# x of pair 0 through SyncE's queue as float32, first weights behind pair 0's C, GpSimd's other loads spread out

## The chip, the cores and the metric

The kernel runs on one core of one Trainium2 chip. The time is device microseconds of one execution. The core has five engines that run side by side: TensorE (PE in the profile, its weight loads PEld), VectorE (DVE), ScalarE (ACT), GpSimd (POOL) and SyncE (SP). SyncE, ScalarE and GpSimd issue DMAs; each has a queue of its own, and all queues run on the same 16 DMA engines. Of the three, only GpSimd's DMAs change the type of the data on the way.

## The reference

Two parts follow each other. The first is a chunked state-space recurrence (Mamba2) over x, a, B and C with 4 batches, 8 heads, 768 tokens, head width 32 and state width 16. The second is a bilinear feed-forward layer on its result, with 3,072 tokens, 256 model columns and 1,536 hidden columns.

```python
for c in range(S // chunk):
    cum = np.cumsum(la, axis=-1)                       # la: log of a in this chunk
    L = np.exp(cum[:, :, :, None] - cum[:, :, None, :]) * causal
    y_intra = ((Cc @ Bc^T) * L) @ xc
    y_inter = (Cc @ state) * np.exp(cum)[..., None]
    y[:, :, sl] = y_intra + y_inter
    state = np.exp(la.sum(-1)) * state + sum_j decay_j * outer(Bc_j, xc_j)
...
x2 = y.transpose(0, 2, 1, 3).reshape(B * S, H * D)
out = ((x2 @ w_a) * (x2 @ w_b)) @ w_out
```

## The kernel before, in words

The kernel takes chunks of 128 tokens: six blocks, and in each block two pairs of batches, so that pair p is block p // 2 and batches 2 (p % 2) and the one after it. Pairs 0 and 1 (block 0) start the work and have a path of their own; pairs 2 and 3 (block 1) and the later ones follow with other layouts.

For a pair of block 0 the work is this. `load1` brings B, C or x of one batch (64 partitions of two tokens each). `scan` on VectorE makes the running products of a; `factors_mm` and a reciprocal turn them into factors per token. `scale_bc` multiplies B or C with its factor into float16 (tiles bm and cm). `transposes` turns bm and cm on TensorE, VectorE and ScalarE copy the result to bt and ct. `scores` forms B times C in four banks (SC), `mask` multiplies them with the causal table: three quarters on VectorE, one by a ScalarE copy to tmp and a GpSimd product. `pv_u` multiplies the masked scores with x (tile X16, called xn in the profile), and `evac0` or `pv1` copies the result to X2T. Then the feed-forward part begins on TensorE: `unit_mm` multiplies X2T with a slice of Wa or Wb, `evac_a` copies the first product, `times` multiplies the two, `out_mm` multiplies with Wo. Warm-up products of constants fill TensorE's early gaps.

The order of instructions on each engine is written out by hand; no scheduler moves them. An engine runs its list in order and waits where an instruction's inputs are not there. The loads at the start are spread over the queues as follows:

- SyncE: a, then of pair 0 half of B and a quarter of C, then of pair 1 half of C and half of B. Later `load_q(1)`, C and B of block 1 in eight DMAs (tiles cq and bq), which wait until the first Wa has landed; then x of pairs 2 and 3 as float32 (`load_x32`, cast by ScalarE at L723), B of pairs 2 and 3, and block 2.
- ScalarE: the other half of B, half of C and a quarter of C of pair 0 (L198, rows 32 to 63 of batch 0), and the other halves of C and B of pair 1.
- GpSimd, after it has built the identity and the causal table: x of pair 0 in two DMAs, cast to float16 on the way, the first half of Wa (`w0`) and of Wb, x of pair 1 in two DMAs, the second half of Wa. It then computes `mid_rows(0, 1)` (tile Ps, used from the first `turned_rows` on) and its share of pair 0's mask, clears two tiles and issues the second half of Wb.

The weights are float32 in memory and are cast to float16 by GpSimd's queue. The columns of a half that a unit uses: units 0 to 2 of each pair use the first half of Wa and Wb, units 3 to 5 the second.

The DMAs of SyncE and ScalarE share eight completion semaphores in turn, so an issue waits until the DMA eight places before it, in the order of the program, has landed.

Of the kernel before, what the change touches and what calls it, by code (L numbers as in the profile page):

```python
# [10 lines left out]
f32 = mybir.dt.float32  # L11
# [5 lines left out]
AFTER = mybir.DependencyInfo(mybir.DependencyClass.Sync, mybir.DependencyReason.DATA)  # L17
# [11 lines left out]
def kernel(  # L29
# [13 lines left out]
    nc = tc.nc  # L43

    nb, H, S, D = x.shape
# [32 lines left out]
    Wa = [big.tile([128, 2, KC], f16, name=f"Wa{t}") for t in range(2)]  # L78
    Wb = [big.tile([128, 2, KC], f16, name=f"Wb{t}") for t in range(2)]
# [27 lines left out]
    in32 = ctx.enter_context(tc.tile_pool(name="in32", bufs=2))  # L107
# [16 lines left out]
    st = {}  # L124
# [4 lines left out]
    def bank(name):  # L129
        return psf.tile([128, 512], f32, name=name, tag=f"ff{next(banks)}")  # L130
# [9 lines left out]
    def by_token(t_):  # L140
        return t_.rearrange("p h r n -> p (h r n)").rearrange("p (t h n) -> p t h n", t=2, h=H)

    def load1(eng, p, which, bt, i0=0, n=64, to=None):
        blk, bp = divmod(p, NBP)
        if p >= P2:
            return eng.dma_start(
                by_token(pair_in[p][which])[:, bt],
                (B, C, x)[which][2 * bp + bt, :, blk * Q : (blk + 1) * Q, :].rearrange("h q n -> q h n"),
            )
        src = (B, C, x)[which][2 * bp + bt, :, blk * Q + 2 * i0 : blk * Q + 2 * i0 + 2 * n, :]  # L150
        if to is None:
            to = pair_in[p][which]
        return eng.dma_start(  # L153
            to[64 * bt + i0 : 64 * bt + i0 + n].rearrange("i h r n -> i h (r n)"),
            src.rearrange("h (i r) n -> i h (r n)", r=2),
        )
# [23 lines left out]
    def load_w(half, W):  # L180
        src = moe_w_a if W is Wa else moe_w_b
        c = slice(half * KC, (half + 1) * KC)
        return nc.gpsimd.dma_start(W[half], src.rearrange("(f p) e -> p f e", p=128)[:, :, c])

    def load_wo(half):
# [2 lines left out]
            moe_w_out.rearrange("(g p kk) e -> p g (kk e)", p=128, kk=3)[:, 2 * half : 2 * half + 2],  # L188
        )

    nc.sync.dma_start(a_sb, a.rearrange("b h (k q) -> (b h) k q", q=Q))
    for p_ in range(2):
        tiles(p_)
# [1 line left out]
    load1(nc.sync, 0, 0, 0)  # L195
    load1(nc.scalar, 0, 1, 1)
    load1(nc.sync, 0, 1, 0, 0, 32)
    load1(nc.scalar, 0, 1, 0, 32, 32)  # L198
    for w in (1, 0):
        load1(nc.sync, 1, w, 0)  # L200
        load1(nc.scalar, 1, w, 1)
# [19 lines left out]
    for bt in range(2):  # L221
# [1 line left out]
        nc.gpsimd.affine_select(  # L223
            out=v, in_=v, compare_op=ALU.is_ge, fill=0.0, base=0, pattern=[[-1, 2], [1, Q]], channel_multiplier=-2
        )
    for p in range(2):
        for bt in range(2):
            load1(nc.gpsimd, p, 2, bt)
        if p == 0:
            w0 = load_w(0, Wa)  # L230
            load_w(0, Wb)
    load_w(1, Wa)

    def warmup(bank, *widths):
        for cols in widths:
            nc.tensor.matmul(
                bank[:, 0:cols],
                nc.const_aps.tensor(1.0, [128, 128], mybir.dt.bfloat16),
                nc.const_aps.tensor(1.0, [128, cols], mybir.dt.bfloat16),
                start=True,  # L240
                stop=True,
                skip_group_check=True,
            )


    def scan(lo, hi):
        for k in range(lo, hi):
            nc.vector.tensor_tensor_scan(Pr[:, k], a_sb[:, k], zero, 1.0, ALU.mult, ALU.add)
# [4 lines left out]
    def sel_over_mid(lo, hi, eng):  # L253
        eng.tensor_tensor(
            out=selr[:, lo:hi].rearrange("p k t c -> p k (t c)"),
            in0=sel.rearrange("p t b h -> p (t b h)").unsqueeze(1).broadcast_to((BH, hi - lo, 2 * NBP * H)),
            in1=rmid[:, lo:hi].unsqueeze(2).broadcast_to((BH, hi - lo, 2 * NBP * H)),
            op=ALU.mult,
        )
# [24 lines left out]
    def mid_rows(lo, hi, eng):  # L284
        k = slice(lo + NBLK - NT, hi + NBLK - NT)
        eng.tensor_tensor(
            out=Ps[:, lo:hi], in0=Pr[:, k], in1=rmid[:, k].unsqueeze(2).broadcast_to((BH, hi - lo, Q)), op=ALU.mult
        )

    def clear(t_, eng):  # L290
        words = t_.rearrange("p c s -> p (c s)").bitcast(u32).rearrange("p (g w) -> p g w", g=3)
        eng.memset(words[:, 0:2, 32:96], 0)
# [23 lines left out]
    def flat(f, lo, hi):  # L316
        return f[:, lo:hi].rearrange("p k r b h -> p (k r b h)")
# [47 lines left out]
    def transposes(p, ps=None, between=None, apart=False):  # L365
        s = st[p]
        if ps is None and apart:
            ps = [SC[0], SC[1]]
        TB, TC = (TT[:, 0:256], TT[:, 256:512]) if ps is None else [t_.bitcast(f16)[:, 0:256] for t_ in ps]
        for T_, src in ((TB, s["bm"]), (TC, s["cm"])):  # L370
            for r in range(2):
                nc.tensor.transpose(
                    T_[:, r * 128 : (r + 1) * 128], src[:, r].rearrange("p h n -> p (h n)"), ident
                )
            if between:
                between()
                between = None
        BT = mid.tile([128, 2, 2, Q], f16, name="bt", tag="bt")
        CT = mid.tile([128, 2, Q], f16, name="ct", tag="ct")
        co, ci = CT.rearrange("p t q -> p (t q)"), TC  # L380
        if p < P2:
            co, ci = CT.rearrange("p t (i r) -> p r (t i)", r=2), TC.rearrange("p (r c) -> p r c", r=2)
        b_ = nc.vector.tensor_tensor(
            out=BT.rearrange("p e r k -> p e (r k)"),
            in0=TB.unsqueeze(1).broadcast_to((128, 2, 256)),
            in1=par.unsqueeze(2).broadcast_to((128, 2, 256)),
            op=ALU.mult,
        )
        c_ = nc.scalar.copy(co, ci)
        if apart:  # L390
            tc.declare_no_dep(c_.ins, b_.ins.name, reason="reads of two banks")
        if p < P2:
            BT = BT.rearrange("p e r (t i) -> p e r t i", t=2)
        s["BT"], s["CT"] = BT, CT
# [37 lines left out]
    def product0(m2, e):  # L432

        return (
            st[0]["T1"][:, 2 * m2 : 2 * m2 + 2].rearrange("p m (e r) q -> p e m (r q)", e=2)[:, e],
            (SC0, SC1)[m2][:, :, e * 256 : e * 256 + 256],
            causal.rearrange("p r q -> p (r q)").unsqueeze(1).broadcast_to((128, 2, 2 * Q)),
        )

    def mask(out_in, by_pool=False):  # L440
        o_, i_, c_ = out_in
        if by_pool:
            tmp = mid.tile([128, *c_.shape[1:]], f32, name="tmp", tag="tmp")
            nc.scalar.copy(tmp, i_)  # L444
            nc.gpsimd.tensor_tensor(out=o_, in0=tmp, in1=c_, op=ALU.mult)  # L445
        else:
            nc.vector.tensor_tensor(out=o_, in0=i_, in1=c_, op=ALU.mult)  # L447
# [176 lines left out]
    def unit(p, k2, between=None, by_pool=False):  # L624
        a_ps = unit_mm(p, k2, Wa)
        if between:
            between()
        b_ps = unit_mm(p, k2, Wb)
        asb = evac_a(a_ps)
        return lambda: times(p, k2, b_ps, asb, by_pool)  # L630
# [85 lines left out]
        if blk < NBLK:  # L716
            load_q(nc.sync, blk)

    def load_x32(p):
        x32 = in32.tile([128, H, 2, D], f32, name="x32", tag="x32")  # L720
        for bt in range(2):
            load1(nc.sync, p, 2, bt, to=x32)
        return lambda: nc.scalar.copy(  # L723
            st[p]["X16"].rearrange("p h r d -> p (h r d)"), x32.rearrange("p h r d -> p (h r d)")
        )

    def loads_x(p):
        if p < NP:
            load2(nc.gpsimd, p, 2)
# [52 lines left out]
    scale_bc(0, 1, nc.vector, v.rearrange("p (r b h) -> p r b h", r=2, b=NBP)[:, :, 0])  # L782
    over_mid(1, 2)
    sel_over_mid(1, 2, nc.vector)
    mid_rows(0, 1, nc.gpsimd)
    tb, tcp = bank("tb"), bank("tc")
    transposes(0, [tb, tcp], lambda: warmup(SC[3], 256))
    nc.scalar.copy(flat(fC, 0, 1), v)
    scan(3, 4)
    warmup(SC[3], 512, 512)  # L790
    scores(0)
# [1 line left out]
    mask(product0(0, 1))  # L793
    mask(product0(1, 1), by_pool=True)
    mask(product0(1, 0))
    clear(planes[0], nc.gpsimd)
    warmup(tcp, 512)
    factors_mm(1, 2, fps, 1)
# [16 lines left out]
    for p in (2, 3):  # L815
        tiles(p)
    x_in = [load_x32(p) for p in (2, 3)]
    for p in (2, 3):
        load2(nc.sync, p, 0)
# [72 lines left out]
    h = unit(1, 4, lambda: scores(2))  # L892
# [32 lines left out]
    for c in range(3):  # L925
        p, bt = divmod(c, NBP)
# [135 lines left out]
```

## Time and profile before

| what | value |
|---|---|
| time, median of 3 runs | 123.13 us (122.97 to 123.83) |
| the profiled execution | 123.47 us, of which the span of the instructions is 121.8 us |
| granted TensorE clock | 1.00 |
| TensorE busy | 116.0 us, 95% of the span |
| VectorE, ScalarE, GpSimd busy | 90.3, 66.7, 58.6 us |
| chain that ended last | PE 68%, DMA 15%, SPq 10%, POOL 3% |
| GpSimd's queue (q0) | 20,256 packets, 3.67 MB |
| SyncE's queue (q1) | 36,976 packets, 7.87 MB |
| ScalarE's queue (q10) | 2,528 packets, 0.36 MB |

How to read the profile: the page cuts the span into 40 equal slices of 3.05 us and gives each engine's busy share of a slice in tenths. The chain of work that ended last is followed back from the last instruction, at each step to what released it. The timeline lists instructions in order of time, alike ones merged, each with its start, its duration, its engine ("SPq", "ACTq" are issues by a queue's engine, not work), its line and its tiles, and in brackets the idle time of the engine before it and what ended that. Line numbers are those of the kernel before; the times are from the start of the span. The DMA view of a stretch of time gives for each queue the packets that started in it, their bytes in MB and the time that they took as a share of 16 engines.

### The profile page before, as it was taken

Reading aid. Unit: us, or ns where it says so; the run is one execution under the profiler, and the core shown is the slowest. Engines: PE = TensorE matmul, PEld = TensorE weight load, DVE = VectorE, ACT = ScalarE, POOL = GpSimd, SP = SyncE. Lnnn points to the kernel's source line nnn. Section 1 sums busy time; section 2 is a strip of 40 time slices with the busy share of each in tenths; the row PEclk is TensorE's granted clock in tenths of the full one; section 3 lists DMA queues with packets and bytes.
Section 4 is the critical chain, followed back from the end, with each engine's and each line's share of the span. In section 5 each row is a group of like instructions: output and inputs, shape, how many; then the busy total and the mean of one; then the engine's idle time right before and its main releaser. Section 6 shows DMA issues by size and latency. Waiting matters only on the chain.

```text
span 121.8 us, 3551 instructions
## 1 busy us (share of the span) xinstructions
PE 116.0 (95%) x1385; PEld 73.6 (60%) x1386; DVE 90.3 (74%) x167; ACT 66.7 (55%) x131; POOL 58.6 (48%) x94
## 2 busy tenths in 40 slices
PE   7889899999999999999999999999999999999990
PEld 2336689888734468644476464766464684655880
DVE  5998986999888995599966989686799345748000
ACT  0446746668567654567656637545645537565220
POOL 7994876987769999395901995200000000000000
DMA  3999999993488999999992909212001012010122
GB/s 65 131 172 193 205 200 181 172 201 73 102 85 98 168 104 107 123 78 114 197 309 95 95 0 122 12 46 86 5 0 43 12 51 74 0 43 0 43 97 81
DMA packets 59777, 12.13 MB, mean 100 GB/s; under 512 B 54992, under 2 KB 59728, under 8 KB 59760
## 3 DMA queue, kind: packets, MB, share of 16 engines
q0 software_dynamic: 20256, 3.67, 42.8%
q1 hardware_dynamic: 36976, 7.87, 35.8%
q10 hardware_dynamic: 2528, 0.36, 1.8%
q8 instruction: 11, 0.18, 0.7%
q14 instruction: 6, 0.05, 0.2%
HBM read 12.42 MB, written 3.15 MB: 128 GB/s over the span
## 4 chain that ended last, share of the span: by engine, by line
PE 68%; DMA 15%; SPq 10%; POOL 3%; issue 1%; DVE 0%; ACT 0%; POOLq 0%
PE ops L691 22%; PE aps L665 20%; PE bps L665 20%; DMA cq<-in_C_dram 7%; SPq L161 5%; DMA Wa<-in_moe_w_a_dram 5%; SPq L153 4%; DMA bq<-in_B_dram 3%; PE SC L402 2%; PE SC L471 2%; POOL xn L153 1%; PE SC L534 1%; POOL causal L223 1%; POOL planes L344 1%; DVE turned L357 0%
## 5 line engine op out<-in xcount | busy, mean ns | idle before, releaser
L610 ACT COPY asb<-aps 128x512 f32<-128x512 f32 x72 | 41.9, 587 | 18.3 <-PE aps L665 13.9
L677 DVE TENSOR_TENSOR hkb<-bps,asb 128x512 f16<-128x512 f32 x60 | 40.1, 685 | 12.4 <-ACT asb L610 11.3
L665 PE MATMUL bps<-XB,Wb 128*128 128x512 f16 x120 | 35.7, 379 | 0.2 <-ACT asb L610 0.2
L665 PE MATMUL aps<-XB,Wa 128*128 128x512 f16 x120 | 35.7, 379 | 0.0
L691 PE MATMUL ops<-Wo,hkb 128*128 128x256 f16 (+1 forms) x252 | 28.1, 268 | 0.0
L691 PEld LDWEIGHTS <-hkb 128*128 128x128 f16 x252 | 23.0, 98 | 3.8
L665 PEld LDWEIGHTS <-Wb 128*128 128x128 f16 x120 | 12.4, 103 | 13.9 <-issue 0.5
L665 PEld LDWEIGHTS <-Wa 128*128 128x128 f16 x120 | 12.1, 103 | 11.7 <-issue 0.5
L447 DVE TENSOR_TENSOR t<-SC,causal_q 128x512 f16<-128x512 f32 x27 | 17.3, 681 | 2.4 <-PE SC L402 2.4
L703 ACT ACTIVATE osb<-ops 128x256 f32<-128x256 f32 (+1 forms) x20 | 7.6, 380 | 18.4 <-PE ops L691 18.4
L445 POOL TENSOR_TENSOR t<-tmp,causal_q 128x512 f16<-128x512 f32 x5 | 5.8, 1160 | 8.8 <-ACT tmp L444 8.8
L175 POOL DMA_DIRECT2D xn<-in_x_dram x8 | 9.5, 1193 | 0.0
L344 POOL TENSOR_TENSOR planes<-bq,FB 128x256 f16<-128x256 f32 x10 | 7.7, 774 | 1.6 <-DMA bq<-in_B_dram 1.5
L620 DVE TENSOR_TENSOR hk<-bps,asb 128x512 f16<-128x512 f32 x11 | 7.3, 677 | 1.6 <-ACT asb L610 0.9
L344 POOL TENSOR_TENSOR planes<-cq,FC 128x256 f16<-128x256 f32 x10 | 7.6, 775 | 1.3 <-DMA cq<-in_C_dram 1.1
L447 DVE TENSOR_TENSOR t<-SC,causal 128x512 f16<-128x512 f32 x11 | 7.0, 676 | 0.4 <-PE SC L402 0.3
L596 PE MATMUL aps<-X2T,Wa 128*128 128x256 f16 x48 | 6.8, 274 | 0.3 <-ACT G L858 0.3
L444 ACT COPY tmp<-SC 128x512 f32<-128x512 f32 x10 | 5.9, 589 | 1.8 <-PE SC L402 1.4
L556 ACT ACTIVATE XB<-SC 128x512 f16<-128x512 f32 (+1 forms) x9 | 4.6, 548 | 4.1 <-PE SC L499 2.4
L596 PE MATMUL bps<-X2T,Wb 128*128 128x256 f16 x48 | 6.6, 273 | 0.0
L445 POOL TENSOR_TENSOR t<-tmp,causal 128x512 f16<-128x512 f32 x5 | 5.7, 1157 | 0.6 <-ACT tmp L444 0.5
L357 DVE STREAM_TRANSPOSE turned<-planes 128x384 f32<-128x384 f32 x10 | 5.5, 564 | 0.5 <-POOL planes L344 0.5
(100 smaller groups left out, 107.3 us busy)
## 6 DMA issues: line engine op xcount, KB each, us to landing
out_dram<-osb SPq DMA_DIRECT2D x23, 128.0 KB, 2.0
cq<-in_C_dram SPq DMA_DIRECT2D x20, 64.0 KB, 4.1
bq<-in_B_dram SPq DMA_DIRECT2D x20, 64.0 KB, 4.0
bn<-in_B_dram SPq DMA_DIRECT2D x8, 128.0 KB, 4.8
xn<-in_x_dram POOLq DMA_DIRECT2D x8, 128.0 KB, 5.7
Wa<-in_moe_w_a_dram POOLq DMA_DIRECT2D x2, 384.0 KB, 7.9
Wb<-in_moe_w_b_dram POOLq DMA_DIRECT2D x2, 384.0 KB, 8.5
Wo<-in_moe_w_out_dram POOLq DMA_DIRECT2D x2, 384.0 KB, 5.8
```

What stands on the lines that cost most here:

```text
L153: return eng.dma_start(to[64 * bt + i0 : 64 * bt + i0 + n].rearrange("i h r n -> i h (r n)"), src.rearrange("h (i r) n -> i h (r n)", r=2),)
L175: eng.dma_start(by_token(pair_in[p][which]).rearrange("p t h n -> p (t h) n"), src.rearrange("t h q n -> q (t h) n"))
L344: eng.tensor_tensor(out=plane[:, c0 : c0 + 4 * step].rearrange("p (j c) s -> p j s c", c=step)[:, :, :, 0:N], in0=by_batch[blk][which][:, ...
L445: nc.gpsimd.tensor_tensor(out=o_, in0=tmp, in1=c_, op=ALU.mult)
L447: nc.vector.tensor_tensor(out=o_, in0=i_, in1=c_, op=ALU.mult)
L596: nc.tensor.matmul(ps[:, kk * 2 * Q : (kk + 1) * 2 * Q], W[k // 6][:, f, k % 6 // 3 * 384 : (k % 6 // 3 + 1) * 384].rearrange("p (c kk) -> ...
L610: (nc.vector.tensor_copy if on_dve else nc.scalar.copy)(asb, a_ps)
L620: eng.tensor_tensor(out=s["hk"][:, 2 * k2 : 2 * k2 + 2, :].rearrange("p k q -> p (k q)"), in0=b_ps, in1=asb, op=ALU.mult)
L665: nc.tensor.matmul(t_, W[k // 6][:, f, k % 6 // 3 * 384 : (k % 6 // 3 + 1) * 384].rearrange("p (c kk) -> p kk c", kk=3)[:, k % 3], XB[:, b ...
L677: return lambda: nc.vector.tensor_tensor(out=s["hk"][:, k], in0=ps[1], in1=asb, op=ALU.mult)
L691: nc.tensor.matmul(o_ps[:, 0:w], hk[:, k, c * Q : (c + 1) * Q], Wo[:, k, cs], start=(k == 0), stop=(k == NK - 1), skip_group_check=True,)
L703: nc.scalar.activation(out=o_sb[:, 0:w], in_=o_ps[:, 0:w], func=AF.Copy, scale=1.0 / (YS * YS))
```

## The change

`load_x32` is moved up, and x of pair 0 goes through it: two DMAs of SyncE's queue into a float32 tile, right behind SyncE's quarter of C of pair 0 and ahead of its halves of C and B of pair 1. The cast to float16 (`x0()`) becomes a ScalarE copy between the copy to fC and the copy to tmp of pair 0's mask. On GpSimd, the first half of Wa waits until ScalarE's quarter of C of pair 0 (`c0`) has landed; behind it come the first half of Wb and the first x DMA of pair 1. The second x DMA of pair 1, the second half of Wa and `mid_rows(0, 1)` stand behind GpSimd's mask of pair 0. The work on VectorE and TensorE keeps its order.

```diff
+    def load_x32(p):
+        x32 = in32.tile([128, H, 2, D], f32, name="x32", tag="x32")
+        for bt in range(2):
+            load1(nc.sync, p, 2, bt, to=x32)
+        return lambda: nc.scalar.copy(
+            st[p]["X16"].rearrange("p h r d -> p (h r d)"), x32.rearrange("p h r d -> p (h r d)")
+        )
...
     load1(nc.sync, 0, 1, 0, 0, 32)
-    load1(nc.scalar, 0, 1, 0, 32, 32)
+    c0 = load1(nc.scalar, 0, 1, 0, 32, 32)
+    x0 = load_x32(0)
     for w in (1, 0):
         load1(nc.sync, 1, w, 0)
         load1(nc.scalar, 1, w, 1)
...
-    for p in range(2):
-        for bt in range(2):
-            load1(nc.gpsimd, p, 2, bt)
-        if p == 0:
-            w0 = load_w(0, Wa)
-            load_w(0, Wb)
-    load_w(1, Wa)
+    w0 = load_w(0, Wa)
+    tc.add_manual_dep(w0.ins, c0.ins.name, AFTER, reason="first weights behind pair 0")
+    load_w(0, Wb)
+    load1(nc.gpsimd, 1, 2, 0)
...
-    mid_rows(0, 1, nc.gpsimd)
     tb, tcp = bank("tb"), bank("tc")
     transposes(0, [tb, tcp], lambda: warmup(SC[3], 256))
     nc.scalar.copy(flat(fC, 0, 1), v)
+    x0()
     scan(3, 4)
...
     mask(product0(1, 0))
+    load1(nc.gpsimd, 1, 2, 1)
+    load_w(1, Wa)
+    mid_rows(0, 1, nc.gpsimd)
     clear(planes[0], nc.gpsimd)
```

More of the change, by code (lines that the diff above doesn't have):

```diff
@@ L717, in loads_q @@
             load_q(nc.sync, blk)
[L719 to L725, printed above, removed]
     def loads_x(p):
```

## The prediction

> **What bounds the kernel now.** I read the page's slices of the span first, then the chain of waits, then the timeline up to 38 us, then the DMA queues by windows.
>
> The slices show two stages. The DMA engines are full from about 3 to 28 us; TensorE is busy to the end.
>
> ```profile
> PE   7889899999999999999999999999999999999990
> DMA  3999999993488999999992909212001012010122
> ```
>
> The chain that ended last runs through the DMA queues before it is TensorE alone:
>
> ```profile
> 2.56 1.49 POOL xn L153 x2
> 4.06 6.40 DMA Wa<-in_moe_w_a_dram
> 10.46 0.02 issue
> 10.47 0.32 SPq L161
> 10.79 0.04 issue
> 10.84 8.20 DMA cq<-in_C_dram
> ...
> 30.96 3.40 DMA bq<-in_B_dram
> ```
>
> From 35.92 us on its pieces are matmuls back to back, so a change in the first 10 us reaches the end only through what TensorE loses or regains before that. The timeline shows the point where three things arrive together (columns: start, duration, engine, line, operation, tiles, idle time before with its releaser):
>
> ```profile
> 3.32 0.64 SPq L153 DMA_DIRECT2D bn<-in_B_dram  x1
> 3.60 0.65 ACTq L153 DMA_DIRECT2D bn<-in_B_dram  x1
> 7.17 0.59 ACT L444 COPY tmp<-SC 128x512 f32<-128x512 f32 x1 [0.62 <-PE SC L402]
> 9.89 0.43 DVE L331 TENSOR_TENSOR bm<-bn,fB 128x256 f16<-128x256 f32 x1
> 10.24 0.28 DVE L563 TENSOR_SCALAR X2T<-py 128x128 f16<-128x128 f32 x1
> 10.37 0.11 PEld L372 LDWEIGHTS <-bm 128*128 128x128 f16 x2 [0.66 <-DVE bm L331]
> 10.56 0.81 PEld L596 LDWEIGHTS <-Wa 128*128 128x128 f16 x8
> 22.53 0.48 PEld L402 LDWEIGHTS <-turned 32*64 32x64 f16 x32 [0.38 <-DVE turned L357]
> ```
>
> B of pair 1 is scaled at 9.89: ScalarE's half of it, issued at 3.60, took 6.3 us and landed at 9.87; SyncE's half, issued at 3.32, took 4.4 us. Pair 1's transposes wait for it at 10.37. Wa (4.06 + 6.4 = 10.46) arrives when X2T is ready (10.52). So **pair 1's B and the first weights are due at the same moment, with 0.1 us to spare**.
>
> Last, how queues share the engines. In 24 to 26 us GpSimd's queue carried the second half of Wo and SyncE's carried B:
>
> ```profile
> q0 software_dynamic: 213, 0.33, 96.2%
> q1 hardware_dynamic: 203, 0.03, 16.5%
> ```
>
> One for one, though a weight packet (1,536 B, 134 ns in the trace's packet records) lasts ten times a 128 B one (13 ns). SyncE's queue gets 102 packets a us there; from 14.0 to 15.5 us it is 135 against 178, 90 a us. Alone, from 26.4 to 27.4, it moved 1,521 in one us. **Rows of B behind weights move some fifteen times slower than rows without them.**
>
> **The change, part by part.**
>
> *x of pair 0.* Removed from GpSimd's queue: two issues (0.87 and 0.69 us) and 1,024 packets that last 31 ns each with the cast; added to SyncE's: two issues of 0.64 us (what x of pair 2 takes, at L153) and 1,024 packets of 256 B at 20 to 22 ns (805 passed between 22 and 23 us). That is 1,024 x 10 ns / 16 engines = 0.64 us less DMA work. The issues stand at 2.67 and 3.35, where C and B of pair 1 stood; the packets follow C's at 4.4. Beside ScalarE's queue (1,024 packets of B and C at 13 ns) they need (1,024 x 20 + 1,024 x 13) ns / 16 = 2.1 us, so x lands about 6.5 to 7.0.
>
> The cast on ScalarE is one copy of 128x512 to float16, 0.62 us (the two at L723 lasted 614 and 621 ns). It stands ahead of the copy to tmp at 7.17, behind which idle time of 0.62 us shows: it fits if x lands by 6.55; a landing at 7.0 holds tmp, and with it GpSimd's mask, back by 0.45 us. That mask ran 8.01 to 9.16, since mid_rows (7.65, 0.39 us) stood before it; mid_rows now comes after, worth 0.25. Together 0 to +0.2 us on the second half of pair 0, covered by the later wait below; without that cover it would cost up to 0.2.
>
> *Pair 1 behind x.* An issue on SyncE or ScalarE waits for the landing of the DMA eight before it (the waits of SyncE's queue show it: x of pairs 2 and 3 at L153 waits for cq, 2.6 us in all). SyncE's C of pair 1 thus waits for ScalarE's C of pair 0 (1.54 + 3.1 = 4.63) and goes out at 4.65 instead of 2.67; B goes out at 5.33 instead of 3.32, **2.0 us later**.
>
> *First weights behind C of pair 0.* That half C is issued at 2.23 and takes 2.7: it lands at 4.98. Wa goes out at 5.05 instead of 4.06. GpSimd has nothing queued behind this wait that is due before the mask near 8. A weight DMA's first packet comes 1.5 us after its issue (Wo: 16.89 to 18.36, 21.68 to 23.21), so at 6.55. Before it was 6.6, since Wa queued behind x. So weights start when they did; with x gone from their queue they fill it sooner, Wa landing about 9.8 and Wb 11.9 instead of 12.48.
>
> *Where they meet.* B's rows from SyncE cannot start before 5.33 + 1.5 = 6.8 (1.5 is 0.81 to 2.30, first packet of ScalarE's B). Weights are then on the engines, 512 packets of Wa and Wb without a break. I let 100 of B's 512 packets slip through while the weights come up; 412 at 102 a us take 4.0 us; 0.5 more to land (last packet 9.39, landing 9.87, for ScalarE's half) makes 11.3, and up to 0.6 for the tail of C ahead of it: **11.6 us against 9.87, +1.75**. Bounds: weights half a us slower to come up, and B lands near 9.4, at no cost; half of C's 512 rows also caught, and it is 13.0 (+3.1; behind Wb come x's 128 B packets, which let the rest through). I take 11.6, as the 203 and 135 packets are of just this meeting.
>
> *What stands behind it.* On VectorE the scaling at 9.89 is followed by X2T (10.24) and bt (10.81); on TensorE the transposes are followed by pair 0's first products. All slip by 1.75: bt, scores(1), three masks, pv1, X2T, the products of pair 1 at 15.08. TensorE has no long wait from there to 22.15. At 22.53 it waits 0.38 us for turned, which hangs on cq and on GpSimd (idle 1.14 us before 19.89), not on pair 1: that 0.38 is given back. Near 35.9 I count 0.1 more, as bq's landing at 34.36 does not move with pair 1. GpSimd's other issues (x of pair 1's second half at 9.2, Wa's second half at 9.9 instead of 6.83, Wb's at 11.6 instead of 9.40) cost nothing: their queue has Wa, Wb and x ahead until about 12.5, and the products that need them begin at 18.33 and 19.64, against landings of 16.3 and 18.8 before.
>
> **Sum:** 1.75 - 0.38 - 0.1 = +1.25 us. The profiled execution took 123.47 us (span 121.8 and 1.7 around it); it would take 124.7. The median of the three runs is 0.34 lower, 123.13, so I forecast **124.4 us**.
>
> One page speaks to the meeting. The Trainium skill, "DMA: Bandwidth & Descriptors", section "Queues, rings and completion order", says that an engine goes round its queues a packet at a time, a packet being typically some 9 to 17 descriptors. If B's small rows went in such groups, B's 32 rows per engine would pass in two to four turns and be on time (the first rival below). The 213 against 203 records of 24 to 26 us say one row a turn.
>
> **Rivals.**
>
> *Pair 1 in time, a small gain.* For it: weights come up slowly where small packets are still about (87 records of their queue from 7 to 8 us, against 286 in the two us after 8.5), and ScalarE's halves of C and B no longer meet x's cast packets. It decides if B lands by 9.9. Then what is left is 0.64 us of DMA work, of which TensorE can take back the 0.38 before scores(2): 123.13 - 0.4 = 122.7. Against it: 1,521 rows a us fell to 102 in the one meeting of B with weights, and SyncE's B took 5.7 to 6.4 us there; from 5.33 that is 11.0 to 11.7.
>
> *C and B both caught.* C's rows from SyncE (4.65 + 1.5 = 6.15) stand behind x's until about 6.3. If x ends 0.4 later, half of C goes at the slow rate too, and B lands at 13.0: +3.1 - 0.5 = +2.6, 125.7 us. It decides once C lands after 8.98, when VectorE scales it. For it: cq, issued into weights at 10.47, had its first packet only at 14.07. Against it: the C halves of pair 1 took 3.9 us before, and 4.65 + 3.9 = 8.55.
>
> *x too late for its users.* If x landed after 8.0, pair 0's products at 8.17 would wait. Until 11.6 that is hidden behind B's wait, so it changes no number unless the first rival holds, where it costs up to 0.5: 123.2.
>
> **How the numbers follow.** Forecast 0.55, the first rival 0.30 (with the late x in it), the second 0.15. A measurement of this kernel tells about 1% (1.2 us) from no change. The forecast's +1.25 lies on that edge: of its 0.55, 0.36 is slower by over 1% (B at 11.6 or later, or less given back), 0.19 within. The first rival is within 1% for 0.25; 0.05 is left for faster, since the gain would have to exceed all DMA work saved. The second is slower. That gives 0.05, 0.44, 0.51. The range runs from 122.7, the first rival, to 125.8, just over the second.
>
> **What would show it.** Right: SyncE's C and B of pair 1 issued near 4.65 and 5.33; Wa near 5.05; B's issue to landing 5.7 us or more; the scaling of B at L337 near 11.6 and the transposes behind it, with TensorE idle over 1 us there; the wait of 0.38 at scores(2) gone; x's cast near 6.6 to 7.2. Wrong: B landed before 9.9, or a wait after 12 us that grew (for Wb, cq or turned), or a gap of TensorE after 22 us that took the delay up.

## The result and the profile after

The changed kernel takes 124.84 us (median of 11 runs, 123.72 to 125.21) against 123.37 us of the kernel before on the same chip (11 runs): a ratio of 1.0096, 95% interval 1.0072 to 1.012, or +1.2 us (the medians differ by 1.5). A ratio leaves out the executions that took over 1.5% longer than the fastest of the same kernel (two of six in e5, for one), while the medians given are over all. The changed kernel's profiled execution took 124.87 us, with a span of 123.2 us against 121.8, so the two traces compared here differ by 1.4 us. The granted clock is 1.00 in both. The size was forecast (124.4), but the wait that was to make it, for B of pair 1, is not there.

The slices of the changed kernel:

```profile
PE   7799799999998999999999999999999999999990
DMA  3999999997657999899992739911101012010122
```

TensorE is at 7 in the fifth slice (12.3 to 15.4 us; 8 before) and dips to 8 in the thirteenth (37 to 40). On the DMA engines the dip behind 28 us is now 7, 6, 5, 7 where 3, 4, 8, 8 stood: the same loads, later and more spread. At 8 to 9 us, where a slice is too coarse to show it, half of the engines' time was free: 38 weight packets passed then, and 129 in the next us.

The chain that ended last (start, duration, what):

```profile
2.24 3.19 DMA cn<-in_C_dram
5.42 0.31 issue
5.73 0.89 POOL Wa L183
6.62 0.71 POOL Wb L183
7.33 8.03 DMA xn<-in_x_dram
15.37 0.04 issue
15.41 0.67 PE SC L462 x32
...
31.52 4.34 DMA bq<-in_B_dram
```

Where x of pair 0 and Wa stood, there now stand C of pair 0, the issues of Wa and Wb behind it, and **x of pair 1, which lands 8 us after its issue**. The timeline (start, duration, engine, line, operation, tiles, idle time before and what ended it; line numbers are 6 higher than before at these places):

```profile
5.48 0.64 SPq L153 DMA_DIRECT2D bn<-in_B_dram  x1
5.73 0.89 POOL L183 DMA_DIRECT2D Wa<-in_moe_w_a_dram  x1 [3.17 <-DMA cn<-in_C_dram]
7.45 0.62 ACT L195 CAST xn<-x 128x512 f16<-128x512 f32 x1 [0.65 <-DMA x<-in_x_dram]
8.71 1.16 POOL L451 TENSOR_TENSOR t<-tmp,causal 128x512 f16<-128x512 f32 x1 [0.67 <-ACT tmp L450]
9.23 0.92 DVE L337 TENSOR_TENSOR cm<-cn,fC 128x256 f16<-128x256 f32 x1
9.81 0.73 POOL L153 DMA_DIRECT2D xn<-in_x_dram  x1
10.40 0.39 DVE L337 TENSOR_TENSOR bm<-bn,fB 128x256 f16<-128x256 f32 x1
10.84 0.11 PEld L378 LDWEIGHTS <-bm 128*128 128x128 f16 x2 [0.59 <-DVE bm L337]
11.23 0.78 PEld L602 LDWEIGHTS <-Wa 128*128 128x128 f16 x8 [0.16 <-DMA Wa<-in_moe_w_a_dram]
12.22 0.27 PEld L408 LDWEIGHTS <-bt 32*64 32x64 f16 x32 [0.21 <-DVE bt L389]
15.41 0.42 PEld L462 LDWEIGHTS <-xn 64*32 64x32 f16 x32 [0.90 <-DMA xn<-in_x_dram]
23.85 0.49 PEld L408 LDWEIGHTS <-turned 32*64 32x64 f16 x32 [0.20 <-DVE turned L363]
37.45 0.23 PEld L408 LDWEIGHTS <-turned 32*128 32x128 f16 x16 [1.16 <-DVE turned L363]
```

The same places in the kernel before, as far as they are not shown above:

```profile
8.01 1.15 POOL L445 TENSOR_TENSOR t<-tmp,causal 128x512 f16<-128x512 f32 x1
8.98 0.46 DVE L331 TENSOR_TENSOR cm<-cn,fC 128x256 f16<-128x256 f32 x1
11.58 0.27 PEld L402 LDWEIGHTS <-bt 32*64 32x64 f16 x32 [0.20 <-DVE bt L383]
13.95 0.38 PEld L456 LDWEIGHTS <-xn 64*32 64x32 f16 x32 [0.20 <-issue]
35.91 0.23 PEld L402 LDWEIGHTS <-turned 32*128 32x128 f16 x16 [0.54 <-DVE turned L357]
```

Pair 1's B waits for no DMA: its scaling at 10.40 follows VectorE's own work (SyncE's half landed at 8.53). Wa is issued 1.7 us later than before (4.06) and lands at 11.19 instead of 10.46. Scores of pair 1 begin at 12.22 (before 11.58, +0.64), pv1 at 15.41 (13.95, +1.46), pair 1's next products at 16.58 (15.08, +1.50), scores(2) at 23.85 (22.53, +1.3), scores(4) at 37.45 (35.91, +1.5). So in this execution the whole loss is there at 15.4 us: **0.64 at the scores of pair 1, 0.8 more at the wait for x of pair 1**.

Two things hold the scores at once. Wa lands 0.73 later, but TensorE waits for it only 0.16 us at 11.23, since the transposes ahead of it are late too: 10.84 against 10.37, as VectorE's scaling of C of pair 1 (9.23) took 0.92 us beside GpSimd's mask, which the cast of x had put back. By these rows each of the two alone would have cost about half a us here (in e2, without the cast, the scores are still 0.54 late).

The last line shows why it is not made good later. TensorE came to that wait at 36.29, only 0.9 us behind the kernel before (35.37), and then waited 1.16 us (0.54 before), since the last DMA of bq landed at 35.86 (34.36 before). That DMA was issued 0.56 us later, at 31.52. Of the 16 DMA engines 15 had their part through by 33.70 (33.87 before); one engine's part made the rest of the wait.

### The profile page after: what moved, and what is told of

It is laid out like the page before. It is cut to its first block, busy times and chain, and to the rows that moved or that the text cites. A ratio compares the mean times of both kernels' runs of the same rounds, so it can differ in the third digit from the quotient of the medians.

```text
span 123.2 us, 3555 instructions
## 1 busy us (share of the span) xinstructions
PE 116.4 (95%) x1386; PEld 73.5 (60%) x1386; DVE 90.8 (74%) x167; ACT 67.3 (55%) x132; POOL 57.3 (47%) x92
## 4 chain that ended last, share of the span: by engine, by line
PE 71%; DMA 13%; SPq 8%; POOL 2%; ACTq 1%; issue 1%; ACT 1%; DVE 0%; POOLq 0%
PE ops L697 22%; PE aps L671 20%; PE bps L671 20%; DMA xn<-in_x_dram 7%; SPq L161 5%; DMA bq<-in_B_dram 4%; SPq L153 3%; DMA cn<-in_C_dram 3%; PE SC L408 2%; PE SC L477 2%; PE aps L602 2%; ACTq L153 1%; PE bps L602 1%; PE SC L540 1%; POOL Wa L183 1%
```

## The experiments

Every ratio is against the kernel before on the same chip. A first group, e1 to e4, takes the change apart; e5 to e8 followed from it, and e9 to e11 from those.

### e1: x of pair 1 by SyncE too

```diff
+    x1 = load_x32(1)          # SyncE, behind B of pair 1
-    load1(nc.gpsimd, 1, 2, 0)
-    load1(nc.gpsimd, 1, 2, 1)
+    x1()                      # ScalarE, behind evac0
```

> The changed kernel, but x of pair 1 also comes as float32 through SyncE's queue (behind its half of B of pair 1) and is cast by ScalarE behind evac0; GpSimd's queue then holds Wa and Wb alone. Theory 1 (the loss is made where pair 1's products wait for x of pair 1, which stands behind Wa and Wb in GpSimd's queue and landed at 15.4 to 15.6 us against 13.3 before): x of pair 1 lands near 9 to 10, pv1 starts at 14.6 instead of 15.41, right behind its masks, and the time falls by 0.3 to 0.8 us, to a ratio of 1.002 to 1.007 against the kernel before. Theory 2 (the loss is made at the head, where C of pair 0 landed 0.45 us later behind x and the cast pushed GpSimd's mask back by 0.7 us): pv1 may start earlier, but the time stays at 1.008 to 1.011.

Measured: 128.16 us, ratio 1.041 (1.0372 to 1.0448). x was issued at 6.02 and 6.70, Wa at 5.63, Wb at 6.52; x landed at 11.84 and 14.39, just behind Wa (11.43) and Wb (13.87). ScalarE waited in its place in the list:

```profile
14.47 0.62 ACT L195 CAST xn<-x 128x512 f16<-128x512 f32 x1 [3.95 <-DMA x<-in_x_dram]
```

So rows of SyncE's queue that are issued behind weights do wait for them. The experiment doesn't give the price of a late x of pair 1, since ScalarE's wait also held the copy to ct, and scores(1) began only at 15.48. Neither theory had expected this.

### e2: the cast behind the copy to tmp

```diff
-    x0()                      # ahead of scan(3, 4), scores(0) and the mask's tmp
+    x0()                      # behind mask(product0(1, 0))
```

> The changed kernel, but ScalarE casts x of pair 0 behind the copy to tmp instead of ahead of it. GpSimd's mask then starts near 8.1 instead of 8.71 and no longer runs beside VectorE's scaling of C of pair 1, which should take 0.46 us again instead of 0.92. Theory 2 (the head): X2T of pair 0 and the transposes of pair 1 come 0.4 us sooner and the time falls by 0.3 to 0.5 us, to 1.005 to 1.007. Theory 1: Wa (11.19), Wb (13.25) and x of pair 1 (15.4) land as in the changed kernel, so pv1 and the end stay: 1.008 to 1.011.

Measured: 124.04 us, ratio 1.0046 (1.0022 to 1.007).

```profile
8.16 1.16 POOL L451 TENSOR_TENSOR t<-tmp,causal 128x512 f16<-128x512 f32 x1
9.24 0.42 DVE L337 TENSOR_TENSOR cm<-cn,fC 128x256 f16<-128x256 f32 x1
11.13 0.78 PEld L602 LDWEIGHTS <-Wa 128*128 128x128 f16 x8 [0.57 <-DMA Wa<-in_moe_w_a_dram]
```

The mask runs 0.55 us earlier and C's scaling takes 0.42 instead of 0.92, but the first products still wait for Wa, so 0.1 us is gained there. The rest of the gain is at pv1, which begins at 14.6: the second x DMA of pair 1, which stands behind the mask on GpSimd, goes out at 9.26 instead of 9.81 and lands at 14.70 instead of 15.55. That the earlier issue made it land earlier is not shown, as 15 of the 16 engines had it by 14.04 here and by 13.98 in the changed kernel; the difference is in the last engine's part. The time is that of theory 2, but not the whole path: X2T and the transposes came 0.5 us sooner, and the weights kept the rest back.

### e3: x of pair 0 back on GpSimd's queue, wait and spread kept

```diff
-    x0 = load_x32(0)
-    x0()
+    for bt in range(2):       # GpSimd, ahead of Wa
+        load1(nc.gpsimd, 0, 2, bt)
```

> The changed kernel with x of pair 0 back on GpSimd's queue, ahead of Wa and cast on the way; the wait for C of pair 0 and the spread of GpSimd's issues stay. Wa goes out at 5.05 to 5.1 instead of 5.73. Theory 1: Wa, Wb and x of pair 1 come 0.3 to 0.7 us sooner than in the changed kernel, x of pair 1 at 13.3 to 14.5: ratio 1.000 to 1.005. Theory 2: pair 0's C lands at 4.98 again and the cast is gone, ratio 0.998 to 1.002. If it stays at 1.008 or more, moving x of pair 0 is innocent, and the wait and the spread cost it all.

Measured: 124.02 us, ratio 1.0047 (1.0024 to 1.007). C's quarter lands at 4.93, as before, instead of 5.42, and Wa goes out at 5.21. Wa lands at 10.42 and pv1 begins at 13.9, both as before. So the numbers of theory 1 came, and still 0.6 us is lost. What the trace shows of it is later: Wo's two DMAs took 7.4 and 6.5 us (before 5.5 and 6.0), and the first products with XB begin at 32.15 (31.89). That the one made the other is not shown, and the profiled execution is only 0.2 us longer than that of the kernel before (span 121.95 against 121.77).

### e4: no wait for C

```diff
-    tc.add_manual_dep(w0.ins, c0.ins.name, AFTER, reason="first weights behind pair 0")
```

> The changed kernel without the wait of the first Wa for pair 0's C: GpSimd issues Wa and Wb from 2.6 us on. Theory 1: Wa lands near 8, Wb near 10 and x of pair 1 near 11, so pv1 waits for no DMA; but x, C and B on SyncE's queue now meet the weights (one packet for one), x of pair 0 lands at 9 or later instead of 7.4, and pair 0's products wait for it: between 1.003 and 1.02, by what x costs. Theory 2, if the wait for C were the whole loss and the meeting cost nothing: 1.000 to 1.003.

Measured: 129.83 us, ratio 1.0532 (1.0497 to 1.0567). Wa goes out at 2.51, 0.16 us ahead of x of pair 0, and x lands at 9.46 and 12.69 instead of 6.07 and 7.42:

```profile
12.71 0.62 ACT L195 CAST xn<-x 128x512 f16<-128x512 f32 x1 [5.95 <-DMA x<-in_x_dram]
```

With x on SyncE the wait for C is needed: without it the kernel loses 5 us more, far over the 1.02 that was expected at most.

### e5 and e6: the weights 0.3 and 0.5 us earlier

```diff
-    load1(nc.scalar, 0, 1, 1)
+    ch = load1(nc.scalar, 0, 1, 1)          # ScalarE's half of C, lands first
-    tc.add_manual_dep(w0.ins, c0.ins.name, ...)
+    tc.add_manual_dep(w0.ins, ch.ins.name, ...)
```

e6 has the cast behind tmp as well.

> The changed kernel, but the first weights wait for ScalarE's half of C of pair 0 (landed 4.83) instead of its quarter (5.43), so Wa goes out at about 5.1, where the prediction put it, instead of 5.73. Theory of the prediction (weights are on the engines 1.5 us after their issue, so at 6.6, and B of pair 1 meets them): B lands at 9.5 to 11.5, its scaling is the wait ahead of pair 1's transposes, and the time stays or rises (124.8 to 126). Rival (weights need about 1.6 us to the first packet and some 1.5 more to come up, and SyncE's rows are through by 8): B still lands by 9.2, Wa near 10.5 to 10.7, x of pair 1 near 14.8; the time falls by 0.4 to 0.6, to 124.2 to 124.4.

> The same wait for ScalarE's half of C, and the cast of x of pair 0 put behind the copy to tmp. If the two losses at the head (the weights' later issue, and the cast ahead of tmp) are separate, both go: scores(1) at 11.6 (12.22 in the changed kernel, 11.58 before), x of pair 1 near 13.5 to 14.5, time 123.4 to 123.9. If only the weights count, it equals the run with the wait alone; if B meets the weights after all, it is 124.8 or more.

Measured: e5 125.45 us, ratio 1.0107 (1.0065 to 1.015); e6 125.12 us, ratio 1.0107 (1.007 to 1.0144). The rival of e5 fell, and of e6 the last case came. The timeline of e5:

```profile
5.42 0.88 POOL L183 DMA_DIRECT2D Wa<-in_moe_w_a_dram  x1 [2.86 <-DMA cn<-in_C_dram]
5.77 0.64 SPq L153 DMA_DIRECT2D bn<-in_B_dram  x1
11.64 0.58 DVE L337 TENSOR_TENSOR bm<-bn,fB 128x256 f16<-128x256 f32 x1 [0.92 <-DMA bn<-in_B_dram]
12.28 0.11 PEld L378 LDWEIGHTS <-bm 128*128 128x128 f16 x2 [1.77 <-DVE bm L337]
```

B of pair 1 landed at 11.55, and at 11.57 in e6: **the meeting that the prediction put at 11.6**. In e5 its price by the ratio is hardly more than that of the changed kernel, as the late x of pair 1 is then hidden behind it: scores(1) at 13.48 is 1.26 later than in the changed kernel, pv1 at 15.99 only 0.6 later. With the cast out of the way the meeting is the dearer one: e6 stands at 1.0107, e2, which has the same cast and no meeting, at 1.0046 (the intervals just meet). How the queues shared the engines in e5, from 8 to 9 us and from 10 to 11 us (packets, MB, share of 16 engines):

```profile
q0 software_dynamic: 82, 0.13, 71.4%
q1 hardware_dynamic: 8, 0.00, 0.7%
...
q0 software_dynamic: 92, 0.12, 73.1%
q1 hardware_dynamic: 426, 0.05, 37.7%
```

Here SyncE's rows do not go one for one: hardly any pass until Wa is nearly through, and then, summed over the 16 engines, between four and five go for one weight packet. One for one does occur elsewhere: in e4, from 5.5 to 7.0 us, 154 weight packets passed and 158 rows.

### e7: x of pair 1 ahead of the weights

```diff
+    for bt in range(2):
+        load1(nc.gpsimd, 1, 2, bt)          # ahead of Wa and its wait
-    load1(nc.gpsimd, 1, 2, 0)
-    load1(nc.gpsimd, 1, 2, 1)
```

with the cast behind tmp.

> The changed kernel with the cast behind tmp, and both DMAs of x of pair 1 on GpSimd's queue ahead of the first weights' wait, instead of one behind Wb and one behind the first mask. Theory that x of pair 1 behind Wb makes the wait of 0.9 us at pv1: that wait goes (x lands by 9), pv1 follows its masks near 13.9, and scores(2) begins near 22.9 instead of 23.85. Price: its 1,024 packets of 31 ns stand beside C and x of pair 0 (2.0 us of 16 engines), so C of pair 0 lands 0.3 to 0.8 later and Wa goes out near 6.2 and lands near 11.5. Sum: 123.6 to 124.6. Rival (Wa and Wb set the order anyway): scores(1) and bps later by as much as x is earlier, no change against the run with the cast alone (124.0).

Measured: 126.45 us, runs of 123.88 to 128.79, too far apart for a ratio; the profiled one took 128.79, at a granted clock of 0.96. In it x of pair 1 landed at 7.34 and 8.68, but C's half of pair 1 came at 9.92 and B at 13.45. Wa was issued at 5.29 and B at 5.32; 15 of the 16 engines had B through by 11.15. Neither expectation came, and what x of pair 1 costs by itself is not told by this run.

### e8: the spread alone, on the kernel before

```diff
     load1(nc.gpsimd, 1, 2, 0)
-    load1(nc.gpsimd, 1, 2, 1)
-    load_w(1, Wa)
...
     mask(product0(1, 0))
+    load1(nc.gpsimd, 1, 2, 1)
+    load_w(1, Wa)
+    mid_rows(0, 1, nc.gpsimd)
```

> The kernel before with one part of the change alone: GpSimd's issues of the second half of x of pair 1, the second half of Wa and mid_rows stand behind the first mask; x of pair 0 stays with GpSimd's queue and the weights wait for nothing. Prediction: this costs nothing (123.4), since that queue has Wa, Wb and x ahead until 12.5. Rival: the run with wait and spread but x of pair 0 on GpSimd's queue had pv1 in time (13.96) and still took 0.6 us more, lost near the first products of the later blocks (32.15 against 31.89); if that loss is the spread's, this run is 123.7 to 124.1 too; if it is the wait's (Wa issued 5.21 instead of 4.06), it equals the kernel before.

Measured: 123.54 us, ratio 0.9985 (0.9957 to 1.0013). The spread costs nothing on the kernel before. So e3's 0.6 us comes with the wait, though Wa landed in time there; by which path is not shown.

### e9: the changed kernel again

> The changed kernel once more, to see on which side of the meeting it stands. In its first profile SyncE's B of pair 1 was issued at 5.48 and the weights at 5.73, and B landed at 8.5; with the weights at 5.42 or 5.21 and B at 5.77 or 5.56 it landed at 11.6. Theory now (whichever of the two is issued first wins): B ahead of Wa again and landed by 9.2, time 124.3 to 125.2, clock 1.0. Rival (the order is luck from run to run): B at 11 or later in this profile, time up to 126.

Measured: 124.59 us, ratio 1.0074 (1.0041 to 1.0107). B was issued at 5.67, Wa at 5.89, and B landed at 8.79: in time again. The loss is split in another way than in the first profile: scores(1) at 12.51, 0.9 later than before, and only 0.3 more by the wait for x (pair 1's next products at 16.31). The chain of this execution goes from the cast over tmp and the mask to the second x DMA of pair 1:

```profile
7.54 0.62 ACT xn L195
8.15 0.49 ACT tmp L450
8.69 0.10 issue
8.79 1.10 POOL t L451
9.89 5.38 DMA xn<-in_x_dram
```

So the cast and x of pair 1 hang together: what holds the mask holds the issue of x. That this makes the landing late is not shown, as 15 of the 16 engines had x by 14.53, ahead of the end of the masks (14.98), and the last at 15.27.

### e10: the weights later still

```diff
-    tc.add_manual_dep(w0.ins, c0.ins.name, ...)
+    tc.add_manual_dep(w0.ins, first32[0].ins.name, ...)   # first x DMA of pair 0
```

> The changed kernel with the first weights waiting for the first DMA of x of pair 0 (landed 6.07) instead of C's quarter (5.43), so Wa goes out near 6.3 to 6.5 and surely behind SyncE's B. Theory (late weights are the whole loss on this side, 1 us of time for 1 us of issue, as Wa to landing takes 5.5): B in time, Wa lands near 11.8 to 12.0, scores(1) near 12.9, x of pair 1 near 15.5 to 16, time 0.4 to 0.8 above the changed kernel, 125.2 to 125.6. Rival (weights can't come up before small rows are through at 8, whenever they are issued): Wa lands at 11.2 as before and the time is unchanged at 124.8.

Measured: 125.07 us, ratio 1.0117 (1.007 to 1.0163), 0.5 us above e9 in medians, though the intervals overlap.

```profile
6.41 0.89 POOL L183 DMA_DIRECT2D Wa<-in_moe_w_a_dram  x1 [3.85 <-DMA x<-in_x_dram]
11.99 0.78 PEld L604 LDWEIGHTS <-Wa 128*128 128x128 f16 x8 [0.86 <-DMA Wa<-in_moe_w_a_dram]
```

The rival fell: Wa lands at 11.95, 5.5 us after its issue, as in the changed kernel. On this side a later issue is a later landing, one for one.

### e11: the spread undone

```diff
+    for bt in range(2):
+        load1(nc.gpsimd, 1, 2, bt)          # behind Wb
+    load_w(1, Wa)
...
+    mid_rows(0, 1, nc.gpsimd)               # ahead of the mask, as before
```

> The changed kernel with one part undone: the second half of x of pair 1 and the second half of Wa are issued right behind Wb and the first half again, and mid_rows stands where it did before. Theory: the queue order is Wa, Wb, x either way, so x of pair 1 lands as late (15 to 15.5) and the time is the changed kernel's, 124.5 to 125. Rival (x of pair 1 is late because its second half is issued at 9.8): x lands by 14, pv1 follows its masks, time down by 0.5 to 0.8, 124.0 to 124.3.

Measured: 125.78 us, ratio 1.0165 (1.0126 to 1.0205), 1.2 us above e9. Neither expectation met it. x of pair 1 came earlier (13.76 and 14.40), but with Wa held to 5.97, GpSimd's three issues and mid_rows now fill its time to 10.1, and the mask starts behind them:

```profile
9.80 1.73 DVE L256 TENSOR_TENSOR_SCAN Pr<-a_sb,zero 32x128 f32<-32x128 f32 x1
...
10.11 1.14 POOL L453 TENSOR_TENSOR t<-tmp,causal 128x512 f16<-128x512 f32 x1
```

With the wait, the spread saves about 1.2 us; without it, it does nothing (e8). A part of the 1.2 us is the clock's: the granted clock was 0.983 to 0.986 in all six executions, and in the trace it was halved from 12.24 to 15.66, so that the first eight products with Wa took 1.87 us instead of 1.06.

### What decides whether B meets the weights

Issue and landing of SyncE's B of pair 1 and of Wa, in us:

| kernel | B issued | Wa issued | B landed | Wa landed |
|---|---|---|---|---|
| e10 | 5.45 | 6.41 | 8.34 | 11.95 |
| e1 | 5.34 | 5.63 | 8.22 | 11.43 |
| e2 | 5.47 | 5.74 | 8.85 | 11.09 |
| changed | 5.48 | 5.73 | 8.53 | 11.19 |
| e9 (changed) | 5.67 | 5.89 | 8.79 | 11.48 |
| e11 | 5.77 | 5.97 | 9.13 | 11.37 |
| e7 | 5.32 | 5.29 | 13.45 | 11.27 |
| e5 | 5.77 | 5.42 | 11.55 | 11.01 |
| e6 | 5.56 | 5.21 | 11.57 | 10.78 |

B ahead of Wa by 0.2 us or more lands before 9.2; B behind it, even by 0.03, lands behind Wa. It is not Wa's time alone: in e3 Wa goes out at 5.21, as in e6, but B had been issued at 3.32 and landed at 7.93. e5 and e11 have B at the same time, 5.77, and Wa 0.55 apart. Why the order counts is not shown.

The order itself is not luck. In every kernel of the table B goes out 0.66 us behind the landing of ScalarE's half of C, as SyncE's C waits for that landing and B follows C. Wa goes out some 0.3 us behind the landing that it waits for. In e5 and e6 that is the same half, so Wa is 0.35 ahead of B. In the changed kernel, e1, e2, e9 and e11 it is ScalarE's quarter of C, which lands 0.55 to 0.64 behind the half, so Wa is 0.2 to 0.3 behind B. In e7, with x of pair 1 ahead of the weights, the quarter lands only 0.35 behind the half, and the two issues are level.

## Why the prediction was right in size and wrong in cause

**The failed step is "That half C is issued at 2.23 and takes 2.7: it lands at 4.98."** The 2.7 is from the trace of before, where x of pair 0 came by GpSimd's queue and started behind. In the changed kernel x's rows follow on SyncE's queue at once, and C's quarter lands at 5.42; with x back on GpSimd's queue (e3) it lands at 4.93. With it failed the next term: GpSimd's issue came 0.31 us after the landing instead of 0.07, for which the working gave no row. So Wa went out at 5.73 and not 5.05, while SyncE's B went out at 5.48, close to the 5.33 of the working. The prediction had Wa 0.28 us ahead of B; it was 0.25 us behind. That turned the order, and with it went the whole +1.75. Both terms were needed: with the late landing alone, Wa would have gone out at 5.49, level with B.

*Where they meet.* Right as a conditional: with Wa 0.35 ahead, B landed at 11.55 and 11.57 against 11.6. The way there was not right. The 102 packets a us, "one for one", was read from a stretch where both queues had long been at work. e5's rows show 8 against 82 and then 426 against 92. The page "DMA: Bandwidth & Descriptors" of the Trainium skill, section "Queues, rings and completion order", has an engine change its queue after a packet of some 9 to 17 descriptors. The prediction concluded that B would then be on time; that holds only if B's rows go in such groups and the weights one by one. With groups on both sides, an engine's share of Wa (256 packets on 16 engines, 16 each) would be about one turn, by an estimate from the page's figure, and B just behind Wa, as in e5, does not speak against it. Nor do 213 against 203 say "one row a turn", as equal groups give equal counts too.

*Weights.* The first packet came at 7.36, 1.6 us after the issue, against 1.5 in the working. But "they fill it sooner, Wa landing about 9.8" allowed 4.75 us from issue to landing; it took 5.46, and 5.2 to 5.6 in e2, e3, e5, e6, e9 and e10. That term was too small by 0.7; with the issue 0.68 later than in the working, Wa landed at 11.19, 1.4 later than forecast and 0.73 later than before. It is one of the two things that hold the head. By edits, the wait with the spread comes to +0.6 us (e3, 1.0047) and the spread alone to nothing (e8); but e3 had Wa as early as before, so its 0.6 us is not the price of a late Wa.

*The cast.* It was put at 0 to +0.2, "covered by the later wait". x landed at 6.07 and 7.42 instead of 6.5 to 7.0, tmp went from 7.17 to 7.97 and the mask from 8.01 to 8.71, +0.7. The cover was the wait for B, and it wasn't there. Putting the cast behind tmp takes the ratio from 1.0096 (1.0074 in e9, whose interval overlaps) to 1.0046, 0.35 to 0.6 us. Together with e3's 0.6 us for the wait this makes up the loss, as far as the ratios tell.

*GpSimd's other issues.* "Cost nothing" is right for the kernel before (e8), and for the second halves of the weights. For x of pair 1 the working named no landing: it asked when the weights' second halves were due and did not ask that of x. TensorE waited for it 0.90 us in the first profile of the changed kernel and 0.3 us in e9. The issue behind the mask does not explain it. Of the 16 engines 15 had the second x DMA 0.8 to 1.1 us after they had Wb in the changed kernel (13.98), e2 (14.04), e9 (14.53) and e10 (14.91), and no sooner in e11 (14.36), where it was issued 1.0 to 1.6 us earlier. With masks done at 14.7 in the changed kernel that was in time; the last engine's part came at 15.55 (14.70, 15.27, 15.62; 14.40 in e11). The first x DMA was late in the same way: 15 engines had it by 13.62 and the last one at 15.37. Why one engine lags is open. An instruction fetch of 961 ns began at 13.34; that it held that engine is only argued, and in e4 and e7 one engine was 0.7 us behind the others (Wa at 9.04, x at 7.34) long before the first fetch (15.71 and 14.48).

*Given back.* 0.18 of the 0.38 at scores(2) was given back (0.20 is left). "bq's landing does not move with pair 1" is wrong: it moved by 1.5 us, 0.56 of it by a later issue and the rest by one engine's part. SyncE's loads of block 1 wait for Wa, and were issued from 11.21 on instead of 10.47.

*Rivals.* "Pair 1 in time" is what happened, but not with its 122.7: it counted the DMA work saved and not the weights' later issue. "C and B both caught" was seen in e7, where C landed at 9.92 (behind the 8.98 of the condition). That B landed at 13.45 there, near the 13.0 of the working, is one engine's part again; 15 had it by 11.15. What was never counted is that **the changed kernel has losses of its own where the meeting is missed**, and that they come to about the same: 1.0096 without the meeting and 1.0107 with it (e5) are the same within their intervals. That the forecast's size was right is luck. It is not a rule that the two cost the same, as e2 and e6 show (1.0046 and 1.0107).

What stays open is the path of e3's 0.6 us, why Wo's DMAs took 1.9 and 0.5 us longer there, and what makes one DMA engine lag.

## What to carry to other kernels

A landing time read from a trace holds only while the same packets are around it; where an edit moves other rows beside a transfer that something waits for, price that transfer anew. Where two queues' issues lie within a few tenths of a us of each other, ask which comes first, as one place in order was worth 3 us of landing here, and give both orders a price. For each DMA behind a moved wait, ask when its own reader is due, not only the largest one's. And before a late landing is put down to its issue, look whether all 16 engines were late or one.

## What the hardware showed that was not expected

**Issue order across queues.** Rows of SyncE's queue issued just behind a weight DMA of GpSimd's queue landed just behind that DMA (table above, e1 and e4), though the weights' first packet comes 1.6 us after the issue. An issue ahead of the weights is not enough everywhere: in the kernel before, ScalarE's half of B of pair 1 was issued at 3.60, 0.46 us ahead of Wa; 14 engines had it by 8.01 and the last two at 9.28 and 9.87.

**VectorE held by GpSimd's mask.** With both inputs in SBUF, a VectorE instruction that ran beside the mask ended 0.28 us after it in the changed kernel (mask to 9.87, cm to 10.15), in e5 (10.11, 10.39) and in e11 (11.25, the scan to 11.53); they lasted 0.92, 0.92 and 1.73 us, instead of 0.42 and 0.40 alone. VectorE's own masks, with one input in PSUM, ran beside it at 0.63 us each as ever. The Trainium skill, "GPSIMD Engine Reference", section "1. Specifications", says that GpSimd's SBUF interfaces are shared with VectorE and that VectorE instructions with two SBUF inputs contend; the trace agrees, and shows that here the VectorE instruction waits nearly to the end of the mask.

**The clock after a gap.** In e5 TensorE stood idle for 1.28 us before pair 1's transposes and stayed at a granted clock of 1.00; in e6 for 1.65 us, and the clock was halved for 3.4 us (columns: stretch, its length, busy time of PE, PEld, DVE, ACT, POOL, clock, DMA share, GB/s):

```profile
11.00:12.00 1.00, 0.00 (x0) 0.00 (x0) 0.34 (x1) 0.00 (x0) 1.00 (x4) 0.96 1.20 205
12.00:13.00 1.00, 0.85 (x7) 0.74 (x8) 0.49 (x3) 0.20 (x1) 0.36 (x2) 0.50 1.96 162
13.00:14.00 1.00, 1.00 (x6) 0.74 (x5) 0.96 (x3) 0.59 (x2) 0.00 (x0) 0.50 1.24 163
14.00:15.00 1.00, 1.00 (x36) 0.44 (x34) 0.01 (x1) 0.73 (x2) 0.58 (x3) 0.50 1.21 192
15.00:16.00 1.00, 1.00 (x16) 0.87 (x9) 0.84 (x2) 0.89 (x3) 0.19 (x1) 0.83 1.17 210
```

The first eight products with Wa took 1.91 us there against 1.04 in e5. The length of the gap does not decide: in e11 one of 1.23 us was followed by a halved clock too. What differs in these traces is how busy TensorE was in the 3.41 us, the length of such a halved stretch, ahead of the change: 1.90 us in e6 (8.51 to 11.92) and 2.06 in e11 (8.83 to 12.24). In e5 it was 2.69 and 2.65 in the two such stretches around its gap (8.11 to 14.93), as the gap lies across both. Nor is it the same each time: of e5's six executions three had a mean clock of 1.00 (124.22 to 125.38 us) and three of 0.986 (125.53 to 127.23). All 23 executions of the changed kernel had 0.997 or more. So a wait of 1.75 us, as forecast, can cost this too; the sum had no term for it.
